# Two remainder tiles of 64 rows become one of 64 and one of 32, and the second one's weights are fetched at another point

## The chip, the cores and the metric

The kernel runs on one core of a Trainium2 chip. Its time is the device time of one execution in microseconds (us), and several executions are timed. The engines of the core work in parallel, each through its own queue in order: TensorE (PE; its weight loads are listed apart as PEld), VectorE (DVE), ScalarE (ACT), GpSimd (POOL) and SyncE (SP), which here issues most DMA transfers.

## The reference

A linear attention with decay feeds a mixture-of-experts layer in which every token goes to exactly one expert.

```
for b in range(nb):                                  # 12 blocks of 64 tokens, state carried along
    intra = (q @ k.T * Dmask) @ v ; inter = (q * lam_pow) @ kv_state
    kv_state = lam_block * kv_state + (k * rev_pow).T @ v
x = attention output as [3072 tokens, 512]
logits = x @ w_gate + modality_bias[modality_id]
e_idx = argmax(logits) ; gate_w = softmax(logits)[e_idx]
for e in range(8):                                   # w1[e]: 512x1024, w2[e]: 1024x512
    mask = e_idx == e
    out[mask] = gate_w[mask] * (relu(x[mask] @ w1[e]) @ w2[e])
```

With the seeded inputs, running the reference gives 1319, 253, 1494 and 6 tokens to experts 3, 5, 6 and 7, and none to the others. In tiles of 256 that is 5 full tiles and 39 left, 253 left, 5 full and 214 left, and 6 left.

## The kernel before

The first stage walks over 24 chunks of 128 tokens and computes attention, the logits and, for each token, a slot in a list sorted by expert (`inv` in DRAM). The tokens' rows go to `xs` in DRAM.

The second stage works on tiles of up to 256 rows of one expert. A **wide** tile (256 rows) gathers its rows with POOL's indirect DMA into `xg`, turns them on PE, splits rows and weights into a high and a low part (`split`: ACT casts, DVE subtracts; `xh`/`xl`, `w1h`/`w1l`, `w2h`/`w2l`) and takes three matmuls for each product (lines 554, 557, 558): `wide` is the first product, `second` the second. A **thin** tile takes a remainder of few rows. It multiplies in plain float32 and skips the splits. Its two halves of the hidden columns sit in the two 64-column halves of the PE array (`thin_first`, L584; `thin_turn`, L593; `thin_second`, L606).

Tiles 0 and 1 (`EARLY`) are wide and known after half of the tokens (`listA`). Tiles 2 and 3 are the thin ones, tiles 4 to 13 are wide and always run, and more follow under `tc.If`. All from tile 2 on come from `listB`, which `late_list` computes on DVE from the counts while tile 0 runs: a remainder of 1 to 64 rows counts as `few`, the first two such become thin, and every other remainder is rounded up to a wide tile.

Weights land in `raw1` (w1) and `raw2` (w2), 4 loads of 512 KB each; a load that would bring the expert already there is issued with a condition and moves nothing. The second thin tile cannot use them, since they hold the first one's weights: `fetch_both` (L643) loads its w1 into the buffers of `w1h` and its w2 into those of `w1l`, in `run_early`, once tile 1's first product no longer needs these. SP issues in program order. Ahead of those loads it stands at tile 2's w1 loads (L814, L531), which have an explicit wait for the last row gather that `run(0)` issued (`gathered`).

The order on PE around this: tile 1's first product, the transposes of thin tile 2's rows (`turn_few`, L640), tile 1's second product, those of thin tile 3's rows, `thin_first` of both, then `thin_turn`, half of `turn_rows` for tile 4 and `thin_second` for one thin tile after the other, then tile 4's first product. A scheduler orders what nothing in the code ties.

Of the kernel before, what the change touches and what calls it, by code (L numbers as in the profile page):

```python
# [15 lines left out]
P = 128  # L16
# [10 lines left out]
THIN = 2  # L27
# [5 lines left out]
LIST = THIN + MAX_WIDE + 2  # L33
# [5 lines left out]
def linear_attention_moe(tc, qkv, lam, modality, wg, mbias, w1, w2, out):  # L39
    nc = tc.nc  # L40
    with ExitStack() as ctx:
# [379 lines left out]
        def late_list(exA, nA):  # L421
# [10 lines left out]
            upto = const.tile([1, E, E], F32, name="upto")  # L432
            nc.vector.tensor_tensor(out=upto, in0=tri, in1=few.unsqueeze(1).to_broadcast([1, E, E]), op=ALU.mult)
            nth = per_expert("nth")
            nc.vector.tensor_reduce(out=nth, in_=upto, axis=AX, op=ALU.add)
            thins = per_expert("thins")
            nc.vector.scalar_tensor_tensor(out=thins, in0=nth, scalar=float(THIN), in1=few, op0=ALU.is_le, op1=ALU.mult)
# [3 lines left out]
            nc.vector.tensor_tensor(out=wides, in0=wides, in1=thins, op=ALU.subtract)  # L441
# [6 lines left out]
            for nm, num, skip, items in (("T", thins, n2, THIN), ("B", wides, nA, LIST - THIN)):  # L448
                base = const.tile([1, E + 1], F32, name="base" + nm)
                nc.vector.memset(base[:, E:], 0.0)  # L450
                nc.vector.tensor_tensor(out=base[:, :E], in0=ebase, in1=skip, op=ALU.add)
                delta = per_expert("delta" + nm)
                nc.vector.tensor_tensor(out=delta, in0=base[:, 1:], in1=base[:, :E], op=ALU.subtract)
                nc.vector.tensor_tensor(out=delta, in0=delta, in1=num, op=ALU.subtract)
                ends, ex, at = tile_list(num, delta, base[:, 0:1], items, nm)
                here = const.tile([1, items], F32, name="here" + nm)
                nc.vector.tensor_scalar(out=here, in0=sidx[:, :items], scalar1=ends[:, E - 1 :], scalar2=None, op0=ALU.is_lt)
# [3 lines left out]
                if nm == "T":  # L461
                    for i, o in enumerate((0, LIST - 1)):
                        prev, own = exs[:, 0:1], exs[:, o + 1 : o + 2]
                        nc.vector.tensor_tensor(out=own, in0=ex[:, i : i + 1], in1=prev, op=ALU.subtract)
                        nc.vector.scalar_tensor_tensor(out=own, in0=own, scalar=here[:, i : i + 1], in1=prev,
                                                       op0=ALU.mult, op1=ALU.add)
                        nc.vector.tensor_copy(out=ats[:, o : o + 1], in_=at[:, i : i + 1])
                        nc.vector.tensor_copy(out=others[:, o : o + 1], in_=here[:, i : i + 1])
                else:
                    nc.vector.tensor_scalar(out=exs[:, 2:LIST], in0=ex, scalar1=float(E - 1), scalar2=None, op0=ALU.min)  # L470
                    nc.vector.tensor_copy(out=ats[:, 1 : LIST - 1], in_=at)
                    nc.vector.tensor_copy(out=others[:, 1 : LIST - 1], in_=here)
# [56 lines left out]
        def fetch_w1(er, kw, after=None):  # L529
            for i in range(4):  # L530
                ld = nc.sync.dma_start(out=raw1[i], in_=w1[bass.ds(er, 1), :, i].rearrange("o p k f -> p (o k) f"), **kw)  # L531
                if after is not None:
                    behind(ld, after)

        def fetch_w2(er, kw, after=None):
            for i in range(4):
                ld = nc.sync.dma_start(out=raw2[i], in_=w2[bass.ds(er, 1), :, 2 * i : 2 * i + 2].rearrange("o p f n -> p (o f) n"), **kw)
                if after is not None:
                    behind(ld, after)
# [38 lines left out]
        def thin_first(x, w):  # L578

            hp = ps.tile([P, 2, TT], F32, name="s", bufs=3)  # L580
            for q in range(2):
                for kc in range(KC):
                    for fh in range(2):
                        mm = nc.tensor.matmul(hp[fh * XT : (fh + 1) * XT, q, :], x[:, kc, :], w[2 * fh + q][:, kc, :],  # L584
                                              start=(kc == 0), stop=(kc == KC - 1))
            hn = work.tile([P, 2 * TT], F32, name="hn", bufs=THIN)
            nc.scalar.activation(out=hn, in_=hp.rearrange("p q t -> p (q t)"), func=AF.Relu)
            return hn, mm

        def thin_turn(hn, mm):  # L590
            tp = ps.tile([P, 4, P], F32, name="x", bufs=2)
            for f in range(4):
                behind(nc.tensor.transpose(out=tp[:, f, :], in_=hn[:, f * P : (f + 1) * P], identity=ident), mm, wait=False)  # L593
            hnt = work.tile([P, 4, P], F32, name="hnt", bufs=THIN)
# [3 lines left out]
        def thin_second(idx, hnt, w2):  # L598

            w = DM // 2  # L600
            yp = ps.tile([P, w], F32, name="o", bufs=2)
            for f in range(FC):
                a, b = divmod(f, 2)
                fh, f4 = divmod(f, 4)
# [3 lines left out]
            y = work.tile([P, w], F32, name="yn", bufs=THIN)  # L608
            nc.scalar.activation(out=y, in_=yp, func=AF.Copy, scale=idx[:, 0, 1:2].bitcast(F32))
            to = work.tile([P, 1], I32, name="to", bufs=THIN)  # L610
            nc.vector.tensor_scalar(out=to, in0=idx[:, 0, 0:1], scalar1=2.0, scalar2=half, op0=ALU.mult, op1=ALU.add)
            sc = nc.gpsimd.indirect_dma_start(
                out=out.rearrange("t (n w) -> (t n) w", n=2),
                out_offset=bass.IndirectOffsetOnAxis(ap=to, axis=0),
                in_=y, in_offset=None, bounds_check=2 * N - 1, oob_is_err=False)
# [21 lines left out]
        def turn_few(x, rows):  # L637
            tp = ps.tile([P, KC, XT], F32, name="x", bufs=2)
            for kc in range(KC):
                nc.tensor.transpose(out=tp[:, kc, :], in_=rows[:, kc * P : (kc + 1) * P], identity=ident[:XT, :XT])  # L640
            return nc.vector.tensor_copy(out=x, in_=tp)

        def fetch_both(er, kw):  # L643

            first, second = parts(F32)
            for i in range(4):
                nc.sync.dma_start(out=first[i], in_=w1[bass.ds(er, 1), :, i].rearrange("o p k f -> p (o k) f"), **kw)
            second = [t.rearrange("p k f -> p (k f)").rearrange("p (f n) -> p f n", f=2) for t in second]
            for i in range(4):
                nc.sync.dma_start(out=second[i],  # L650
                                  in_=w2[bass.ds(er, 1), :, 2 * i : 2 * i + 2].rearrange("o p f n -> p (o f) n"), **kw)
            return first, second
# [4 lines left out]
        def parts(dt):  # L657

            return [[work.tile([P, KC, TT], dt, name=f"{nm}{i}", bufs=1) for i in range(4)] for nm in ("w1h", "w1l")]

        w1h, w1l = parts(F32R)
        xg = [const.tile([m, DM], F32, name=f"xg{t}") for t, m in groups(TT)]
        xq = [const.tile([XT, DM], F32, name=f"xq{i}") for i in range(THIN)]
# [4 lines left out]
        xf = [const.tile([P, KC, XT], F32, name=f"xf{i}") for i in range(THIN)]  # L668
        idxA = [const.tile([P, 2, 2], I32, name=f"idxA{i}") for i in range(EARLY)]
        half = const.tile([P, 1], F32, name="half")  # L670
        nc.vector.memset(half, 0.0)
        nc.vector.memset(half[XT:], 1.0)
# [29 lines left out]
        for g in range(0, ng + 2):  # L702
# [50 lines left out]
            elif g == ng + 1:  # L753
                for i in range(1, 4):
# [5 lines left out]
                    (work.tile([P, 4, 2, DM], F32R, name=nm, tag="load", bufs=LOADS) for nm in ("w2h", "w2l")))  # L760
        hh = [work.tile([P, 2, TT], F32R, name=f"hh{i}", tag="pt", bufs=4) for i in range(4)]
# [4 lines left out]
        tiles = [(TT, listA, i) for i in range(EARLY)] + [(XT, listB, 0), (XT, listB, LIST - 1)]  # L766
# [12 lines left out]
        fixed_ones = EARLY + THIN + MIN_WIDE  # L779
        wides = EARLY + THIN  # L780
# [3 lines left out]
        def rows_of(n):  # L784
# [5 lines left out]
            return fetch_rows(idxs[n], XT, to=[xq[n - EARLY]])  # L790

        def run(n):
# [5 lines left out]
            if n + 1 < fixed_ones:  # L798
# [5 lines left out]
                if n > 0:  # L804
                    fetch_w2(*regs(n + 1))
                turn_rows(TT, turned)
                for m in ahead:
                    gathered = rows_of(m)
                if ahead:
                    behind(nc.gpsimd.drain(), gathered, wait=False)  # L810
                for i in range(4):
                    split(raw1[i], w1h[i], w1l[i])
                if n + 2 < fixed_ones:
                    fetch_w1(*regs(n + 2), gathered)  # L814
            second(idx)

        def run_early(n):

            nonlocal w1h, w1l, before
# [12 lines left out]
            mm = thin_second(idxs[EARLY], hnt[0], raw2)  # L832
# [4 lines left out]
            before = thin_second(idxs[EARLY + 1], hnt[1], both[1])  # L837
            w1h, w1l = parts(F32R)
# [11 lines left out]
        with ExitStack() as nest:  # L850
            for n in range(fixed_ones, len(tiles)):
                nest.enter_context(tc.If(count > n - EARLY - THIN))
# [61 lines left out]
```

## Time and profile before

| | us |
|---|---|
| median of 3 timed runs | 424.17 |
| lowest and highest | 424.06, 426.81 |
| the profiled execution: its time | 426.98 |
| its span, first to last instruction | 425.2 |
| PE busy in it | 411.0 (97%) |
| DVE, ACT, POOL busy | 246.0, 187.5, 100.5 |
| mean granted TensorE clock | 0.996 of full |

The rows further below come from that execution. Times in them count from the start of its span. Its time is 1.78 us more than its span and 2.81 us more than the median.

### The profile page before, as it was taken

The page shows a single profiled execution, that of the slowest core. Times are in us where ns is not written, and L with a number is a line of the kernel's source. Part 1 is how long each engine was busy: PE and PEld are TensorE (multiplying, and loading weights), DVE is VectorE, ACT ScalarE, POOL GpSimd, SP SyncE. Part 2 cuts the span into 40 slices and gives each one's busy share as a digit, 9 for nine tenths or more (in the row PEclk, how much of TensorE's full clock was granted, in tenths as well). Part 3 has the DMA queues.
Part 4 walks back from the last instruction along what each step waited for, and adds up shares of the span by engine and source line. Part 5 has one row for each costly group of instructions (what it writes and reads, how often), then busy time and mean ns, then how long its engine had stood idle before and what let it go on. Part 6 is the DMA issues. An engine that isn't in the chain of part 4 may idle for free.

```text
span 425.2 us, 9463 instructions
## 1 busy us (share of the span) xinstructions
PE 411.0 (97%) x3636; PEld 360.5 (85%) x3636; DVE 246.0 (58%) x481; ACT 187.5 (44%) x298; POOL 100.5 (24%) x110
## 2 busy tenths in 40 slices
PE   8999999999989999799999999999999999999994
PEld 4787888888879897479898989999898989898983
DVE  4595968777379870157574563819092836547240
ACT  1222334233377151147473654637281827455330
POOL 3110143623430742022202031111112020200101
PEclk9999999999999999999999999999999999999998
DMA  5999989899930024901204577711102020100101
GB/s 161 399 333 377 344 306 308 253 340 313 376 103 3 27 52 111 368 11 50 77 25 145 186 213 251 226 71 37 65 4 72 26 74 28 66 26 2 51 1 47
DMA packets 35092, 63.00 MB, mean 148 GB/s; under 512 B 7381, under 2 KB 21213, under 8 KB 35040
## 3 DMA queue, kind: packets, MB, share of 16 engines
q1 hardware_dynamic: 17024, 43.08, 29.6%
q0 software_dynamic: 4800, 12.69, 9.0%
q10 hardware_dynamic: 13216, 6.56, 5.2%
q8 instruction: 30, 0.49, 0.5%
q14 instruction: 22, 0.18, 0.2%
HBM read 91.04 MB, written 13.75 MB: 246 GB/s over the span
## 4 chain that ended last, share of the span: by engine, by line
issue 43%; PE 30%; DMA 12%; POOL 7%; POOLq 2%; DVE 2%; SPq 2%; ACT 0%
PE s L224 6%; PE x L285 5%; DMA load<-in_qkv_dram 5%; PE o L273 5%; DMA idx<-inv 4%; POOL out_dram L628 4%; DMA xg<-xs,idx 3%; POOL xg L514 3%; PE o L262 2%; POOLq L810 2%; PE kv L239 2%; PE o L554 2%; PE o L557 2%; PE o L558 2%; PE s L558 2%
## 5 line engine op out<-in xcount | busy, mean ns | idle before, releaser
L554 PE MATMUL s<-xh,w1h 128*128 128x256 f32 x384 | 108.2, 282 | 0.8 <-issue 0.8
L558 PE MATMUL s<-xh,w1l 128*128 128x256 f32 x384 | 108.0, 281 | 0.3 <-DVE w1l L487 0.3
L557 PE MATMUL s<-xl,w1h 128*128 128x256 f32 x384 | 107.9, 281 | 0.0
L487 DVE TENSOR_TENSOR w1l<-raw,w1h 128x1024 fp32r<-128x1024 f32 x48 | 58.1, 1219 | 82.2 <-ACT w1h L486 81.4
L554 PE MATMUL o<-w2h,hh 128*128 128x512 f32 x192 | 75.9, 395 | 0.0
L558 PE MATMUL o<-w2h,hl 128*128 128x512 f32 x192 | 74.9, 390 | 0.0
L557 PE MATMUL o<-w2l,hh 128*128 128x512 f32 x192 | 74.7, 389 | 0.0
L554 PEld LDWEIGHTS s<-xh,w1h 128*128 128x128 f32 x384 | 72.3, 188 | 1.8 <-issue 1.4
L558 PEld LDWEIGHTS s<-xh,w1l 128*128 128x128 f32 x384 | 72.3, 188 | 0.5 <-DVE w1l L487 0.5
L557 PEld LDWEIGHTS s<-xl,w1h 128*128 128x128 f32 x384 | 72.4, 188 | 0.4
L486 ACT CAST w1h<-raw 128x1024 fp32r<-128x1024 f32 x48 | 49.9, 1052 | 24.7 <-PE s L557 24.7
L487 DVE TENSOR_TENSOR w2l<-raw,w2h 128x1024 fp32r<-128x1024 f32 x48 | 58.4, 1217 | 2.1 <-ACT w2h L486 2.0
L486 ACT CAST w2h<-raw 128x1024 fp32r<-128x1024 f32 x48 | 49.9, 1041 | 0.0
L627 ACT ACTIVATE y<-o,idx 128x512 f32<-128x512 f32 x20 | 13.8, 690 | 77.4 <-PE o L558 44.2
L628 POOL DMA_INDIRECT out_dram<-y,idx x20 | 20.3, 1013 | 106.9 <-ACT y L627 95.6
L514 POOL DMA_INDIRECT xg<-xs,idx x20 | 24.1, 1203 | 83.7 <-PE x L547 80.0
L573 DVE SCALAR_TENSOR_TENSOR hl<-s,hh 128x512 fp32r<-128x512 f32 x48 | 32.8, 684 | 17.0 <-ACT hh L572 17.0
L558 PEld LDWEIGHTS o<-w2h,hl 128*128 128x128 f32 x192 | 36.0, 188 | 7.7
L554 PEld LDWEIGHTS o<-w2h,hh 128*128 128x128 f32 x192 | 36.1, 188 | 7.1
L557 PEld LDWEIGHTS o<-w2l,hh 128*128 128x128 f32 x192 | 36.1, 188 | 7.0
L275 ACT COPY xt<-o 128x256 f32<-128x256 f32 x48 | 17.5, 373 | 51.8 <-PE o L273 47.1
L572 ACT ACTIVATE hh<-s 128x512 fp32r<-128x512 f32 x48 | 28.5, 594 | 16.9 <-PE s L558 16.9
(192 smaller groups left out, 495.5 us busy)
## 6 DMA issues: line engine op xcount, KB each, us to landing
raw<-in_w_dram SPq DMA_DIRECT2D x104, 512.0 KB
load<-in_qkv_dram SPq DMA_DIRECT2D x11, 2048.0 KB
xs<-xn ACTq DMA_DIRECT2D x24, 256.0 KB
load<-in_qkv_dram SPq DMA_DIRECT2D x4, 512.0 KB
w1h<-in_w_dram SPq DMA_DIRECT2D x4, 512.0 KB
w1l<-in_w_dram SPq DMA_DIRECT2D x4, 512.0 KB
inv<-pad SPq DMA_DIRECT2D x2, 196.0 KB
inv<-pad SPq DMA_DIRECT2D x2, 192.0 KB
```

Of the source, the lines that this page charges most:

```text
L224: nc.tensor.matmul(sps[hl][:, p, :], kt[r, p, :], qt[r, p, :], start=True, stop=True)
L273: mm = nc.tensor.matmul(op[half][place(p, hl), i, :], vt[:, (2 * p + hl) * D : (2 * p + hl + 1) * D], pts[hl][:, p, :], start=(c == 0 and ...
L285: nc.tensor.matmul(xp[:, j, : P + E], xt[:, p, :], iw[:, p, :], start=True, stop=True)
L486: cp = nc.scalar.copy(out=hi, in_=src)
L487: df = nc.vector.tensor_tensor(out=lo, in0=src, in1=hi.bitcast(F32), op=ALU.subtract)
L514: last = nc.gpsimd.indirect_dma_start(out=(to or xg)[t][:m], out_offset=None, in_=xs[:rows, :], in_offset=bass.IndirectOffsetOnAxis(ap=idx ...
L554: mm = nc.tensor.matmul(out, ah, bh, start=first, stop=False)
L557: nc.tensor.matmul(out, ah, bl, start=False, stop=False)
L558: return nc.tensor.matmul(out, al, bh, start=False, stop=last)
L572: act = nc.scalar.activation(out=hh[i], in_=hp, func=AF.Relu)
L573: nc.vector.scalar_tensor_tensor(out=hl[i], in0=hp, scalar=0.0, in1=hh[i].bitcast(F32), op0=ALU.max, op1=ALU.subtract)
L628: sc = nc.gpsimd.indirect_dma_start(out=out, out_offset=bass.IndirectOffsetOnAxis(ap=idx[:, t, 0:1], axis=0), in_=y, in_offset=None, bound ...
```

## The change

`THIN` becomes `(64, 32)`: thin tile 2 holds up to 64 rows and thin tile 3 up to 32. `late_list` sorts the remainders by size; a 32-row remainder may also take the first place if no larger one wants it. A remainder for which no place is left becomes a wide tile, as before. A 32-row tile uses four column groups of 32 of the PE array. Its first product is 16 matmuls of 256 columns (16 before), its second is 32 of 128 columns (16 of 256 before), and two transposes stand between them (four before).

The second thin tile's w2 goes to `spare`, a third buffer of the attention stage's load pool, and is fetched in `run(0)`. Its w1 still goes to the `w1h` buffers, and is fetched first in `run_early`. `w1l` is no longer used for it. Tile 2's w1 loads lose the wait for the gather.

```diff
-THIN = 2
+THIN = (P // 2, P // 4)
...
             few = per_expert("few")
             nc.vector.tensor_scalar(out=few, in0=rem, scalar1=0.0, scalar2=None, op0=ALU.is_gt)
-            upto = const.tile([1, E, E], F32, name="upto")
...
-            nc.vector.scalar_tensor_tensor(out=thins, in0=nth, scalar=float(THIN), in1=few, op0=ALU.is_le, op1=ALU.mult)
+            nc.vector.scalar_tensor_tensor(out=size[:, 1], in0=rem, scalar=float(THIN[1]), in1=few, op0=ALU.is_le,
+                                           op1=ALU.mult)
+            nc.vector.tensor_tensor(out=size[:, 0], in0=few, in1=size[:, 1], op=ALU.subtract)
...
-        def fetch_w1(er, kw, after=None):
+        def fetch_w1(er, kw, after=None, to=None):
...
         def thin_first(x, w):
-            hp = ps.tile([P, 2, TT], F32, name="s", bufs=3)
-            for q in range(2):
+            m = x.shape[-1]
+            n = P // m
+            hp = ps.tile([P, 4 // n, TT], F32, name="s", bufs=3)
+            for q in range(4 // n):
                 for kc in range(KC):
-                    for fh in range(2):
-                        mm = nc.tensor.matmul(hp[fh * XT : (fh + 1) * XT, q, :], x[:, kc, :], w[2 * fh + q][:, kc, :],
+                    for fh in range(n):
+                        mm = nc.tensor.matmul(hp[fh * m : (fh + 1) * m, q, :], x[:, kc, :], w[4 // n * fh + q][:, kc, :],
...
-        def thin_second(idx, hnt, w2):
-            w = DM // 2
+        def thin_second(m, idx, hnt, w2):
+            n = P // m
+            w = DM // n
...
-                for j in range(2):
-                    mm = nc.tensor.matmul(yp[j * XT : (j + 1) * XT], hnt[:, f4, fh * XT : (fh + 1) * XT],
+                for j in range(n):
+                    mm = nc.tensor.matmul(yp[j * m : (j + 1) * m], hnt[:, f4, fh * m : (fh + 1) * m],
                                      w2[a][:, b, j * w : (j + 1) * w], start=(f == 0), stop=(f == FC - 1))
...
+        spare = work.tile([P, 4, 2, DM], F32, name="spare", tag="load", bufs=LOADS)
...
         def run(n):
...
                     idxs[m] = get_idx(m)
                 if n > 0:
                     fetch_w2(*regs(n + 1))
+                else:
+                    fetch_w2(*fetch_regs(*tiles[EARLY + 1][1:], True), to=spare)
...
-                    fetch_w1(*regs(n + 2), gathered)
+                    fetch_w1(*regs(n + 2), gathered if n > 0 else None)
...
         def run_early(n):
...
             wide(tail)
+            few1 = parts("w1h", F32)
+            fetch_w1(*fetch_regs(*tiles[EARLY + 1][1:], True), to=few1)
             fetch_w2(*regs(EARLY))
-            both = fetch_both(*fetch_regs(*tiles[EARLY + 1][1:], True))
             turn_few(xf[0], xq[0])
             second(idx)
             turn_few(xf[1], xq[1])
             hn, _ = thin_first(xf[0], raw1)
             fetch_w1(*regs(wides))
-            other, mm = thin_first(xf[1], both[0])
+            other, mm = thin_first(xf[1], few1)
...
-            before = thin_second(idxs[EARLY + 1], hnt[1], both[1])
-            w1h, w1l = parts(F32R)
+            before = thin_second(THIN[1], idxs[EARLY + 1], hnt[1], spare)
+            w1h = parts("w1h", F32R)
```

On SP, from the index loads of the thin tiles on. Before (`raw` is w1 in `raw_121` to `124` and w2 in `raw_125` to `128`; `w1h` and `w1l` are tile 3's weights):

```order
L502 DMA idx_2156<-inv 64x2 [waits DMAHW4_49,DMASW3_49]
...
L502 DMA idx_2168<-inv 64x2 [waits DMAHW6_49]
...
L504 DMA idx_2180<-inv 128x2x2 [waits DMAHW0_49]
...
L531 DMA raw_121<-in_w_dram 128x1024 [waits DMAHW1_49,DMASW1_49]
...
L537 DMA raw_125<-in_w_dram 128x1024 [waits DMAHW5_49,DVE_49]
...
L647 DMA w1h_2455<-in_w_dram 128x1024 [waits DMAHW1_49,PE_49]
...
L650 DMA w1l_2459<-in_w_dram 128x1024 [waits DMAHW5_49]
```

After, the same stretch on SP:

```order
L536 DMA idx_2166<-inv 64x2 [waits DMAHW4_49,DMASW3_49]
...
L536 DMA idx_2178<-inv 32x2 [waits DMAHW6_49]
...
L536 DMA idx_2178<-inv 32x2 [waits DMAHW1_49]
...
L538 DMA idx_2192<-inv 128x2x2 [waits DMAHW2_49]
...
L571 DMA spare<-in_w_dram 128x1024 [waits DMAHW3_49,PE_49]
...
L565 DMA raw_121<-in_w_dram 128x1024 [waits DMAHW7_49]
...
L565 DMA w1h_2449<-in_w_dram 128x1024 [waits DMAHW3_49,PE_49]
...
L571 DMA raw_125<-in_w_dram 128x1024 [waits DMAHW7_49,DVE_49]
```

Tile 3's index list takes four loads for two, its w2 (`spare`) moves ahead of tile 2's w1, which no longer waits for a gather (DMASW), and its w1 moves ahead of tile 2's w2. The first `w1h` load shares a semaphore (DMAHW3) with the first `spare` load.

On PE, thin tile 3 and what stands round it. Before (`xf_150` are its rows, `hnt` its turned hidden values, `w1h` and `w1l` its weights):

```order
L640 MATMUL x<-ident,xq_140 128x64 x4
...
L584 MATMUL s<-w1h_2455,xf_150 64x256
...
L606 MATMUL o<-raw_128,hnt 64x256 x4
L593 MATMUL x<-ident,hn 128x128 x4
...
L606 MATMUL o<-w1l_2459,hnt 64x256 x4
```

After, at the same places on PE:

```order
L679 MATMUL x<-ident,xq_140 128x32 x4
...
L620 MATMUL s<-w1h_2449,xf_150 32x256
...
L644 MATMUL o<-raw_128,hnt_2625 64x256 x4
L630 MATMUL x<-ident,hn_2618 128x128 x2
...
L644 MATMUL o<-spare,hnt_2661 32x128 x32
```

The places are the same; what changes is the width of the column group, the number of transposes and the count and length of the second product's matmuls.

## Rows read from the trace of the kernel before

**Rows 1.** Stretches: their bounds, length, busy us (instructions) of each engine, clock, DMA share, GB/s.
```profile
168.29:178.41 10.12, 7.91 (x66) 4.59 (x64) 0.42 (x1) 1.05 (x2) 1.01 (x1) 1.00 0.98 367
...
188.50:211.60 23.10, 23.10 (x154) 21.22 (x153) 15.63 (x17) 12.90 (x17) 6.61 (x6) 1.00 0.21 59
```

**Rows 2.** Timeline of PE, thin tiles: start, us, instruction, [idle before, releaser].
```profile
168.29 3.67 PE L584 MATMUL s<-raw,xf 128*64 128x256 f32 x32
171.79 0.59 PE L584 MATMUL s<-w1h,xf 128*64 128x256 f32 x2
173.80 1.95 PE L584 MATMUL s<-w1h,xf 128*64 128x256 f32 x16 [1.41 <-DMA w1h<-in_w_dram]
176.54 1.94 PE L584 MATMUL s<-w1h,xf 128*64 128x256 f32 x14 [0.80 <-DMA w1h<-in_w_dram]
178.41 0.66 PE L593 MATMUL x<-ident,hn 128*128 128x128 f32 x4
...
179.86 3.67 PE L606 MATMUL o<-raw,hnt 128*64 128x256 f32 x32 [0.35 <-DVE hnt L595]
183.46 0.65 PE L593 MATMUL x<-ident,hn 128*128 128x128 f32 x4
183.95 0.60 PE L547 MATMUL x<-ident,xg 128*128 128x128 f32 x4
184.90 3.67 PE L606 MATMUL o<-w1l,hnt 128*64 128x256 f32 x32 [0.35 <-DVE hnt L595]
...
188.84 0.28 PE L558 MATMUL s<-xh,w1l 128*128 128x256 f32 x1
```

**Rows 3.** Timeline of SP's DMA issues (a group's time includes its waits).
```profile
149.39 3.14 SPq L502 DMA_DIRECT2D idx<-inv  x4
...
162.60 1.69 SPq L531 DMA_DIRECT2D raw<-in_w_dram  x4
...
166.21 2.10 SPq L647 DMA_DIRECT2D w1h<-in_w_dram  x4
```

**Rows 4.** Timeline of PE in the attention stage: matmuls on 64 by 64 cells.
```profile
97.23 0.67 PE L262 MATMUL o<-qd,state 64*64 64x128 f32 x16
97.83 1.09 PE L273 MATMUL o<-pt,load 128*64 128x128 f32 x16
```

**Rows 5.** Timeline of DVE: row copy, turned copy, low part of the next weights.
```profile
168.40 0.42 DVE L641 COPY xf<-x 128x256 f32<-128x256 f32 x1 [9.09 <-PE x L640]
...
184.15 0.69 DVE L595 COPY hnt<-x 128x512 f32<-128x512 f32 x1 [3.30 <-PE x L593]
...
186.15 3.50 DVE L487 TENSOR_TENSOR w1l<-raw,w1h 128x1024 fp32r<-128x1024 f32 x3 [0.26 <-ACT w1h L486]
```

**Rows 6.** Timeline of ACT: high part of the next weights.
```profile
185.07 2.94 ACT L486 CAST w1h<-raw 128x1024 fp32r<-128x1024 f32 x3
```

**Rows 7.** Timeline of DVE: start, the end of the list, tile 1's first low part.
```profile
11.17 1.29 DVE L227 TENSOR_TENSOR pt<-s,dk 128x512 f32<-128x512 f32 x2 [4.86 <-DMA dk<-tab_d]
...
147.25 0.17 DVE L474 TENSOR_SCALAR listB<-ats 1x21 int32<-1x21 f32 x1
150.04 0.69 DVE L573 SCALAR_TENSOR_TENSOR hl<-s,hh 128x512 fp32r<-128x512 f32 x1 [2.63 <-ACT hh L572]
```

**Rows 8.** Timeline of POOL: the first thin gather, tile 4's first scatter.
```profile
153.34 0.99 POOL L514 DMA_INDIRECT xq<-xs,idx  x1 [5.02 <-DMA idx<-inv]
...
207.49 1.04 POOL L628 DMA_INDIRECT out_dram<-y,idx  x1 [4.01 <-ACT y L627]
```

**Rows 9.** Timeline of PE where thin tile 2's rows are turned.
```profile
156.20 0.28 PE L558 MATMUL s<-xh,w1l 128*128 128x256 f32 x1
156.41 0.46 PE L640 MATMUL x<-ident,xq 64*128 64x64 f32 x4
```

**Rows 10.** DMA, 154.5 to 156.4 us: all that moved.
```profile
DMA packets 160, 0.08 MB, mean 43 GB/s; under 512 B 140, under 2 KB 140, under 8 KB 160
```

**Rows 11.** DMA, 156.4 to 158.2 us: all that moved.
```profile
DMA packets 48, 0.01 MB, mean 7 GB/s; under 512 B 45, under 2 KB 45, under 8 KB 48
```

More of the change, by code (lines that the diff above doesn't have):

```diff
@@ L440, in late_list @@
             nc.vector.tensor_tensor(out=wides, in0=wides, in1=few, op=ALU.add)
-            nc.vector.tensor_tensor(out=wides, in0=wides, in1=thins, op=ALU.subtract)
+            for i in range(2):
+                nc.vector.tensor_tensor(out=wides, in0=wides, in1=thins[:, i], op=ALU.subtract)
             exs = const.tile([1, LIST + 1], F32, name="exs")
@@ L447, in late_list, with only @@
             others = const.tile([1, LIST], F32, name="others")
[L448 to L457, printed above, removed]
+            def only(here, at):
@@ L459, in late_list @@
                 nc.vector.scalar_tensor_tensor(out=at, in0=at, scalar=float(EMPTY), in1=here, op0=ALU.subtract, op1=ALU.mult)
                 nc.vector.tensor_scalar(out=at, in0=at, scalar1=float(EMPTY), scalar2=None, op0=ALU.add)
[L461 to L472, printed above, removed]
+            base = const.tile([1, E + 1], F32, name="baseB")
@@ new lines, in late_list @@
+            nc.vector.memset(base[:, E:], 0.0)
+            nc.vector.tensor_tensor(out=base[:, :E], in0=ebase, in1=nA, op=ALU.add)
+            delta = per_expert("deltaB")
+            nc.vector.tensor_tensor(out=delta, in0=base[:, 1:], in1=base[:, :E], op=ALU.subtract)
+            nc.vector.tensor_tensor(out=delta, in0=delta, in1=wides, op=ALU.subtract)
+            items = LIST - len(THIN)
+            ends, ex, at = tile_list(wides, delta, base[:, 0:1], items, "B")
+            here = const.tile([1, items], F32, name="hereB")
@@ new lines, in late_list @@
+            nc.vector.tensor_scalar(out=here, in0=sidx[:, :items], scalar1=ends[:, E - 1 :], scalar2=None, op0=ALU.is_lt)
+            only(here, at)
+            nc.vector.tensor_scalar(out=exs[:, 2:LIST], in0=ex, scalar1=float(E - 1), scalar2=None, op0=ALU.min)
+            nc.vector.tensor_copy(out=ats[:, 1 : LIST - 1], in_=at)
+            nc.vector.tensor_copy(out=others[:, 1 : LIST - 1], in_=here)
+            tail_at = per_expert("tail_at")
+            nc.vector.tensor_tensor(out=tail_at, in0=ebase, in1=n2, op=ALU.add)
@@ new lines, in late_list @@
+            sh = [1, 2, E]
+            found = []
+            for nm, what in (("is", None), ("ex", sidx[:, :E]), ("at", tail_at)):
+                v = thins
+                if what is not None:
+                    v = const.tile(sh, F32, name="pick" + nm)
+                    nc.vector.tensor_tensor(out=v, in0=thins, in1=what.unsqueeze(1).to_broadcast(sh), op=ALU.mult)
+                got = const.tile([1, 2], F32, name="got" + nm)
+                nc.vector.tensor_reduce(out=got, in_=v, axis=AX, op=ALU.add)
+                found.append(got)
@@ new lines, in late_list @@
+            here, ex, at = found
+            only(here, at)
+            for i, o in enumerate((0, LIST - 1)):
+                prev, own = exs[:, 0:1], exs[:, o + 1 : o + 2]
+                nc.vector.tensor_tensor(out=own, in0=ex[:, i : i + 1], in1=prev, op=ALU.subtract)
+                nc.vector.scalar_tensor_tensor(out=own, in0=own, scalar=here[:, i : i + 1], in1=prev,
+                                               op0=ALU.mult, op1=ALU.add)
+                nc.vector.tensor_copy(out=ats[:, o : o + 1], in_=at[:, i : i + 1])
+                nc.vector.tensor_copy(out=others[:, o : o + 1], in_=here[:, i : i + 1])
@@ L637, in turn_few, with parts @@
         def turn_few(x, rows):
-            tp = ps.tile([P, KC, XT], F32, name="x", bufs=2)
+            m = x.shape[-1]
+            tp = ps.tile([P, KC, m], F32, name="x", bufs=2)
             for kc in range(KC):
-                nc.tensor.transpose(out=tp[:, kc, :], in_=rows[:, kc * P : (kc + 1) * P], identity=ident[:XT, :XT])
+                nc.tensor.transpose(out=tp[:, kc, :], in_=rows[:, kc * P : (kc + 1) * P], identity=ident[:m, :m])
             return nc.vector.tensor_copy(out=x, in_=tp)
[L643 to L652, printed above, removed]
         raw1 = [const.tile([P, KC, TT], F32, name=f"raw1{i}") for i in range(4)]
         raw2 = [const.tile([P, 2, DM], F32, name=f"raw2{i}") for i in range(4)]
-        def parts(dt):
-            return [[work.tile([P, KC, TT], dt, name=f"{nm}{i}", bufs=1) for i in range(4)] for nm in ("w1h", "w1l")]
-        w1h, w1l = parts(F32R)
+        def parts(nm, dt):
+            return [work.tile([P, KC, TT], dt, name=f"{nm}{i}", bufs=1) for i in range(4)]
+        w1h, w1l = parts("w1h", F32R), parts("w1l", F32R)
         xg = [const.tile([m, DM], F32, name=f"xg{t}") for t, m in groups(TT)]
-        xq = [const.tile([XT, DM], F32, name=f"xq{i}") for i in range(THIN)]
+        xq = [const.tile([m, DM], F32, name=f"xq{i}") for i, m in enumerate(THIN)]
         for x in xg + xq:
```

80 lines of the change are left out of this document (48 added, 32 removed).

## The prediction

> **What bounds the kernel now.** I read the busy shares first: PE works 411.0 of 425.2 us, so the kernel is a chain of matmuls, and only what PE does or waits for counts. The table of stretches then says where the chain has slack. A wide tile such as the one from 188.50 to 211.60 keeps PE busy for all of its 23.10 us, while the 10.12 us from 168.29 on have PE busy for 7.91 and the DMA engines for 98% [rows 1]. The reader should see there a stage of its own, in which transfers, not matmuls, end last. The granted clock is 1.00 in both stretches [rows 1], so it is no term of the sum.
>
> PE's timeline opens that stage. The first thin tile's first product runs from 168.29 to 171.79: 32 matmul instructions in 3.50 us, 109 ns apart. The second thin tile's same product begins at 171.79 and gives way to the transposes only at 178.41, after 6.62 us [rows 2]. The rows name the weights in `w1h` as what it waited for, 1.41 and 0.80 us; the other 0.91 of the 3.12 us of excess is restarting behind each stop. SP's timeline says why they are late: SP reaches these loads at 166.21, because at 162.60 it was still held in tile 2's w1 loads, by the row gather [rows 3]. From there both matrices of the second thin tile, 4.2 MB, share the DMA engines at 367 GB/s [rows 1].
>
> **First product of the second thin tile.** The change keeps 32 instructions of 256 columns, but on 32 of the 128 columns of the array. In the 64-column form two run side by side, 109 ns apart [rows 2]. If four run side by side, they are 55 ns apart and the product takes 1.75 us; if still only two, 3.50 us. No row shows four column groups that read the same 128 partitions. I take 1.75, because the form nearest to it, two groups, shows no loss, and keep 3.50 as the other end. With weights in time: 6.62 - 1.75 = 4.87 us saved.
>
> Three column groups of 32 gained a factor of 2.38 rather than 3 in a measurement that the Trainium skill gives ("TensorE: Matmul & The Clock Gate", part 3 on packing small matmuls). No run here shows it; four groups at that efficiency would gain 3.17, an estimate by which this product takes 2.2 us and the whole change gives 418.1.
>
> **Are the weights in time?** Four index loads take 3.14 us of SP [rows 3], 0.78 each. Now there are six, and one for tile 4: from 149.39 until about 154.9. The four loads of `spare`, at 0.53 each (2.10 us for four [rows 3]), go out by 157.0, tile 2's conditional ones (1.69 us [rows 3], less the wait) by 158.7, and the w1 loads after that. Each matrix is 2.1 MB, 5.7 us at 367 GB/s [rows 1]. `spare` lands by about 162, and as each w1 load shares a semaphore with a `spare` load and waits for it, w1 lands by about 168. PE needs it at 171.79 [rows 2]: some 4 us in hand, so the stall goes whole.
>
> **Turning between the products.** From 183.46 to 184.90 there are 1.44 us: four transposes (0.49 until 183.95), the transposes of tile 4's rows, and the rest of a wait for the 0.69 us copy of `hnt` [rows 2, 5]. Two transposes fewer save 0.25, and the copy of half the size should cost the 0.42 of the 128x256 copy [rows 5], 0.27 less. That makes 0.92, 0.52 saved.
>
> **Second product.** It takes 3.60 us now (179.86 to 183.46, the first thin tile's [rows 2]). It becomes 64 instructions of 128 columns. Four side by side without loss would be 27 ns apart, 1.75 us in all. Two side by side, as in the attention stage's 128*64 matmuls, are 55 to 68 ns apart (1.09 us for 16 with the last one's tail [rows 4]), 3.5 to 4.4 us. The nearest row is that stage's 64*64 form, which fills four groups of cells: 16 in 0.60 us (97.23 to 97.83 [rows 4]), 37.5 ns apart. At that, 2.40 us, 1.20 saved.
>
> **What is late next.** Tile 4's first product needs `w1l`. ACT's first cast for it starts at 185.07 [rows 6], DVE's subtraction at 186.15, and one takes 1.17 us (3.50 for three [rows 5]), so it stands at 187.32, 3.86 us after the transposes began at 183.46. These casts wait for tile 4's turned rows, which come 0.25 us sooner: 3.61. PE would want it 0.92 + 2.40 + 0.34 = 3.66 us after the same point (the 0.34 from 188.50, where the second product's 3.60 us end, to 188.84 [rows 2]). So ACT and DVE just keep up: a second product quicker than 2.40 us would gain nothing more.
>
> **At nothing.** The list on DVE grows by four instructions of some 0.17 us [rows 7]. DVE is idle for 2.63 us behind it [rows 7]. The sharper edge is SP, which reads the list, loads the indices at 149.39, so that POOL can gather at 153.34 [rows 3, 8]; that gather moves in the stretch up to 156.4 [rows 10], and PE turns the rows at 156.41, 0.21 us behind the matmul before [rows 9]. There are a few tenths in hand at most: price between 0 and 0.7 us, taken as 0, since SP reads one list entry less ahead of the load. DVE's output address for tile 3 waits for two index loads more, about 1.6 us; behind it stand tile 1's last low parts, which PE reads only in the second half of the product it starts at 156.41 plus the transposes. On POOL, tile 6's gather now stands behind tile 4's first scatter (207.49 [rows 8]), but its rows are turned only behind tile 5's first product, which starts at 211.60 [rows 1]. Four memsets more at the start lie between the steps of a chain of dependent multiplications whose result DVE awaits at 11.17 [rows 7]; 0.2 us at most. All later tiles are bound by PE and only move forward.
>
> **The sum.** 4.87 + 0.52 + 1.20 = 6.59 us. The profiled execution would go from 426.98 to 420.4, its span to 418.6. That execution lies 2.81 us over the median, so from the median: 424.17 - 6.6 = **417.6**, 1.6% faster. Differences under about 1%, 4.2 us, can't be told from no change here.
>
> **Rivals.**
> *Only two column groups at a time* (chance 0.21). The array may be unable to stream four float32 operands out of the same partitions; the 64*64 form, with two groups per row half, already falls from 27 to 37.5 ns [rows 4]. Against it speaks the loss-free pairing in the thin tiles [rows 2]. Then the first product stays at 3.50, the second at 3.60 or so, and what remains is 3.12 + 0.52 = 3.6 us: 420.5, within 1%.
> *The weights don't come earlier* (0.03): the chain from `spare` to `w1h` on SP and the semaphores, with gathers in between, eats the 4 us, and the 3.12 us stall stays. Then 3.5 us are gained: 420.7, within 1%.
> *The list delays the first thin gather* (0.05): PE waits ahead of tile 1's second product, up to 0.7 us and as much again by the gather sharing the DMA engines with `spare`; 419.0, still faster.
> *Slower: an eleventh wide tile* (0.03). With places of 64 and 32, two remainders of 33 to 64 rows no longer both fit, and the second becomes a wide tile, 23.10 us [rows 1], while the stall still goes: 424.17 + 23.1 - 6.6 = 440.7. It decides once the smaller remainder exceeds 32 rows. The reference's counts leave 39 and 6, and the gathers agree: 0.08 MB is 39 rows of 2 KB, 0.01 MB is 6 [rows 10, 11].
>
> **Numbers.** The forecast holds 0.68. The two cases near 420.6 hold 0.24, so the range runs from 416.9 (a few tenths below the forecast for the spread of runs, since ACT and DVE cap the gain) to 420.8. Faster by over 1%: 0.68 + 0.05 = 0.73; within 1%: 0.24; slower: 0.03.
>
> **What would show it.** In the changed profile the second thin tile's first product should take about 1.75 us with no wait for DMA on `w1h`; 3.5 us without a wait means that groups of 32 pair only by two. Its second product should take 2.4 us and the 128x256 copy of `hnt` 0.42. The third matmul of tile 4 should start near 182.2; a wait for `w1l` there means ACT and DVE cap the gain. The first `w1h` load on SP should stand near 159 to 162. A gap ahead of the thin rows' transposes near 156.4 means the list or the gather is late, and four `w1h` casts more would mean another wide tile. The forecast is wrong if PE gains idle time behind 182 us.

## The result, and the profile after

In the first measurement the changed kernel takes 419.59 us (median of four runs, 418.97 to 420.36) against 424.56 us before, 5.0 us less between the medians; the ratio is 0.987 [0.983, 0.991], that is 5.3 us (3.6 to 7.1). Two later measurements, beside more runs of the kernel before, gave 0.983 [0.979, 0.986] and 0.985 [0.981, 0.990]. The time lies in the predicted range, 2.0 us above the forecast of 417.6, but two terms of the sum were wrong and cancel in part, as the experiments show.

The profiled execution after takes 419.86 us, its span 418.1, where those of before were 426.98 and 425.2. PE's timeline in the thin stage, beside [rows 2] and [rows 9] (start, us, instruction, count, idle time before and what ended it):

```profile
156.65 0.46 PE L679 MATMUL x<-ident,xq 64*128 64x64 f32 x4 [0.85 <-DMA xq<-xs,idx]
168.16 0.43 PE L679 MATMUL x<-ident,xq 32*128 32x32 f32 x4
168.52 3.67 PE L620 MATMUL s<-raw,xf 128*64 128x256 f32 x32
172.12 1.93 PE L620 MATMUL s<-w1h,xf 128*32 128x256 f32 x32
173.99 0.66 PE L630 MATMUL x<-ident,hn 128*128 128x128 f32 x4
...
175.42 3.67 PE L644 MATMUL o<-raw,hnt 128*64 128x256 f32 x32 [0.34 <-DVE hnt L632]
179.03 0.44 PE L630 MATMUL x<-ident,hn 128*128 128x128 f32 x2
179.30 0.60 PE L581 MATMUL x<-ident,xg 128*128 128x128 f32 x4
179.98 1.95 PE L644 MATMUL o<-spare,hnt 128*32 128x128 f32 x64
181.87 0.38 PE L588 MATMUL s<-xh,w1h 128*128 128x256 f32 x1
...
182.79 0.38 PE L592 MATMUL s<-xh,w1l 128*128 128x256 f32 x1 [0.43 <-DVE w1l L521]
...
205.66 0.28 PE L588 MATMUL s<-xh,w1h 128*128 128x256 f32 x1
```

The second thin tile's first product runs from 172.12 to 173.99 without a stop: 1.87 us, not 6.62. Its second product ends where tile 4 begins, at 181.87: 1.89 us, not 3.60. The third matmul of tile 4 stands at 182.79, not 188.84, behind a new wait of 0.43 us for `w1l`. A second new wait, 0.85 us for the rows `xq`, stands ahead of the first thin transposes.

SP's DMA issues, beside [rows 3] (a group's time includes its waits):

```profile
148.00 3.88 SPq L536 DMA_DIRECT2D idx<-inv  x6
...
153.31 1.94 SPq L571 DMA_DIRECT2D spare<-in_w_dram  x4
156.15 1.32 SPq L565 DMA_DIRECT2D raw<-in_w_dram  x4
158.32 5.09 SPq L565 DMA_DIRECT2D w1h<-in_w_dram  x4
```

The first load of `w1h` is reached at 158.32 instead of 166.21.

To see where the whole 7.1 us between these two spans came from, I cut them at the first thin transposes and at tile 5's first matmul. Up to the transposes: 156.41 before, 156.65 after. From there to tile 5: 55.36 before (to 211.77), 49.01 after (to 205.66), so 6.35 saved. From tile 5 to the end: 213.43 before, 212.44 after, so 1.0 saved where I had expected nothing. 6.35 + 0.99 - 0.24 = 7.1. Two questions were left: why the medians differ by only 5.0, and why tiles that the diff does not touch became quicker.

### The profile page after: what moved, and what is told of

It is laid out like the page before. It is cut to its first block, busy times and chain, and to the rows that moved or that the text cites. A ratio compares the mean times of both kernels' runs of the same rounds, so it can differ in the third digit from the quotient of the medians.

```text
span 418.1 us, 9536 instructions
## 1 busy us (share of the span) xinstructions
PE 404.6 (97%) x3665; PEld 356.4 (85%) x3666; DVE 245.9 (59%) x487; ACT 188.4 (45%) x298; POOL 100.0 (24%) x110
## 4 chain that ended last, share of the span: by engine, by line
issue 44%; PE 22%; DMA 13%; POOL 8%; DVE 6%; POOLq 3%; SPq 3%; ACT 1%; DVEq 0%; ACTq 0%
PE s L224 6%; PE x L285 5%; DMA load<-in_qkv_dram 5%; PE o L273 5%; DMA idx<-inv 4%; POOL out_dram L666 4%; POOL xg L548 3%; DMA xg<-xs,idx 3%; POOLq L844 2%; PE o L262 2%; PE kv L239 2%; DVE w1l L521 1%; SPq L565 1%; DVE w2l L521 1%; PE s L592 1%
```

## The experiments

Each measurement set its kernels beside runs of the kernel before on the same chip. That kernel's median was 426.98 us beside the first four, 424.44 beside the next four and 427.24 beside the last four, so ratios are compared, not times. The first and the last four ran on one chip, the next four on another; the change as it stands was not timed on that other one.

**The change again, and `spare` fetched later.** The first is the changed kernel itself. The second moves one fetch behind the small tile's w1:

```diff
-                else:
-                    fetch_w2(*fetch_regs(*tiles[EARLY + 1][1:], True), to=spare)
...
+            few_er, few_kw = fetch_regs(*tiles[EARLY + 1][1:], True)
+            fetch_w1(few_er, few_kw, to=few1)
+            fetch_w2(few_er, few_kw, to=spare)
```

> The changed kernel once more, beside the experiments on the same chip. By the steps of its trace it should be 5 to 6 us faster than the kernel before: 6.3 us less between the transposes of the second thin tile's rows and the third matmul of tile 4, less the 0.85 us that PE waited for the first thin gather. If instead the 7.1 us by which the two spans differ are the change's, 7 us.

> spare is fetched in run_early, behind the second thin tile's w1, and no longer in run(0). Theory: spare's 2.1 MB and the first thin gather shared the DMA engines, and that is why PE waited 0.85 us for the rows of the first thin tile; the wait falls to 0.1 us or less, spare still lands some 10 us before it is read, and the kernel is 0.8 us faster than the changed one. Rival: the longer list and the two more index loads made the gather late; the wait stays at 0.6 to 0.9 us and the time is the changed kernel's.

Measured: 420.4 us, ratio 0.983 [0.979, 0.986], and 420.22 us, 0.982 [0.980, 0.985]. Neither profile has a wait for `xq`, so the 0.85 us belongs to single executions, and moving the fetch is worth nothing that can be told: the 0.8 us foreseen for it did not come.

**The order alone.** Two 64-row tiles, with the change's list, its `spare` and its order of fetches:

```diff
-THIN = (P // 2, P // 4)
+THIN = (P // 2, P // 2)
...
-            hn = work.tile([P, F // n], F32, name=f"hn{m}", bufs=1)
+            hn = work.tile([P, F // n], F32, name=f"hn{m}", bufs=2)
...
```

> Both thin tiles are of 64 rows, as before the change; list code, spare and the order of the fetches are the change's. Theory, that the transfers and the column groups each pay their own part: the second thin tile's first product runs without a DMA wait in 3.5 us (6.6 before), its second product stays at 3.6, the wait of 0.85 us for the first gather is there; 3.1 - 0.85 = 2.3 us faster than before. Rival, that the earlier weights are the whole gain: 5 us faster.

Measured: 427.91 us, ratio 1.000 [0.998, 1.003], so neither the 2.3 nor the 5 us came. Its profiled execution is the longest of its runs, so only what happens there is read from it, not how large it is on average. PE's timeline, and a table of stretches (bounds, length, busy us and instructions of PE, PEld, DVE, ACT and POOL, granted clock, DMA share, GB/s):

```profile
162.34 0.68 PE L679 MATMUL x<-ident,xq 64*128 64x64 f32 x4 [3.51 <-DMA xq<-xs,idx]
176.73 0.46 PE L679 MATMUL x<-ident,xq 64*128 64x64 f32 x4
```

```profile
158.00:161.00 3.00, 0.84 (x8) 0.63 (x6) 1.38 (x2) 1.14 (x2) 2.39 (x3) 1.00 0.94 325
161.00:164.00 3.00, 1.66 (x7) 1.35 (x8) 0.93 (x2) 0.39 (x1) 0.60 (x1) 0.65 1.00 376
164.00:167.00 3.00, 3.00 (x9) 2.32 (x8) 1.22 (x2) 0.00 (x0) 0.00 (x0) 0.50 1.03 407
167.00:170.00 3.00, 3.00 (x11) 2.40 (x10) 0.00 (x0) 0.00 (x0) 0.00 (x0) 0.71 0.95 373
```

The gather on POOL, and the loads of `spare` on SP:

```profile
156.26 0.98 POOL L548 DMA_INDIRECT xq<-xs,idx  x1 [5.50 <-DMA idx<-inv]
```

```profile
156.29 2.02 SPq L571 DMA_DIRECT2D spare<-in_w_dram  x4
```

Here the rival on the gather came true, at 2.5 times its price (0.7 and as much again): PE waits 3.51 us for `xq` while the DMA engines are 94 to 100% busy, mostly with weights. The gather was issued together with the loads of `spare`, and PE had its rows 6.1 us later (162.34); in three profiles of the change it was issued 0.7 to 1.3 us ahead of them, and PE had them within 4.1 us. With one such profile this order is a likely cause, not a shown one. Behind the idle time the granted clock falls to 0.50, the 1.2 GHz level, and tile 1's second product takes 14.39 us between the two groups of transposes, where it took 11.49 before (156.41 to 167.90).

**The size alone.** Tiles of 64 and 32 rows, their weights fetched as before, into `w1h` and `w1l` and behind the row gather:

```diff
-                    fetch_w1(*regs(n + 2), gathered if n > 0 else None)
+                    fetch_w1(*regs(n + 2), gathered)
...
-            few1 = parts("w1h", F32)
+            few1, few2 = parts("w1h", F32), parts("w1l", F32)
...
+            fetch_w2(few_er, few_kw, to=few2)
```

> The tiles are of 64 and 32 rows, but the second one's weights are fetched as before the change: w1 into w1h and w2 into w1l, behind tile 2's loads, which wait for the row gather. Theory: in the 32-column form each step of the first product reads all four quarters of w1, so it can't start before the last one lands (176.5 in the trace of before) and ends at 178.4, as before: no gain there. The turn gains 0.5 and the second product 1.7, of which tile 4's w1l lets through 1.7 in all; 1.7 us faster than before, no wait for the first gather. Rival, that the two parts simply add: 1.7 more from the first product, 3.5 us faster.

Measured: 424.35 us, ratio 0.992 [0.990, 0.995]. PE's timeline:

```profile
173.89 0.62 PE L620 MATMUL s<-w1h,xf 128*32 128x256 f32 x4
174.81 0.62 PE L620 MATMUL s<-w1h,xf 128*32 128x256 f32 x2 [0.29 <-DMA w1h<-in_w_dram]
176.99 1.91 PE L620 MATMUL s<-w1h,xf 128*32 128x256 f32 x26 [1.56 <-DMA w1h<-in_w_dram]
178.83 0.66 PE L630 MATMUL x<-ident,hn 128*128 128x128 f32 x4
```

The product takes 4.94 us, with the wait for weights in it. The size alone gains 0.8%, the changed kernel beside it 1.7%: with the small tile, early weights do pay. The 0.8%, 2.6 us between the medians, lies between the two expectations (1.7 and 3.5 us), and some 1.3 us of it are not the size's: the later tiles of this kernel run at the change's pace, and its `w1h` lies at the change's place (last group below).

**The order without the collision, and the row gather's wait alone.** The first is the order alone with `spare` late, as above. The second is the kernel before with one condition more:

```diff
-                    fetch_w1(*regs(n + 2), gathered)
+                    fetch_w1(*regs(n + 2), gathered if n > 0 else None)
```

> Two 64-row tiles with the change's list and order of fetches, but the spare weights fetched behind the ones for the first product, not ahead of the first thin gather. Theory (the order has a worth of its own, and the run with the order alone lost it to the 2 MB of spare that shared the DMA engines with the first thin gather): the wait for xq (3.51 us there) is below 0.3 us, the granted clock does not fall behind it, the second thin tile's first product takes 3.5 to 3.6 us without a wait for weights (6.62 us before), and the kernel is 2.6 to 3.6 us faster than before, ratio 0.992 to 0.994. Rival (the order has no worth without the small second tile, since what the earlier weights give is lost at the next wait): ratio 0.998 to 1.002, and a wait of 2 us or more turns up at tile 4's products.

> The kernel before, in which only the loads of weights behind tile 0 no longer wait for the gather of rows. Theory (this wait is one part of what held up the second thin tile's weights): the loads of w1h start near 164.5 us instead of 166.2, the second thin tile's first product shrinks from 6.62 to about 4.9 us, the kernel is 1.4 to 1.9 us faster, ratio 0.9955 to 0.9968. Rival A (the queue is held by the next buffer to come free and not by the gather): the loads of w1h start where they did within 0.3 us, ratio 0.999 to 1.001. Rival B (the wait kept the gather free of the loads): PE waits over 0.8 us for xq, and the kernel is no faster.

Measured: 423.24 us, ratio 0.997 [0.995, 0.999], and 423.97 us, 0.999 [0.997, 1.001]. PE's timeline of the first:

```profile
170.25 3.62 PE L620 MATMUL s<-w1h,xf 128*64 128x256 f32 x32
173.81 0.66 PE L630 MATMUL x<-ident,hn 128*128 128x128 f32 x4
```

SP's DMA issues of the second:

```profile
153.39 1.30 SPq L531 DMA_DIRECT2D raw<-in_w_dram  x4
...
160.37 2.52 SPq L647 DMA_DIRECT2D w1h<-in_w_dram  x4
```

In the two profiles the product takes 3.56 and 3.55 us without a wait, the full 3.1 us less than in [rows 2], and SP reaches `w1h` at 154.45 and 160.37 instead of 166.21. In the second, tile 2's loads stand at 153.39 instead of 162.60, so the row gather was what held SP there, as the prediction read it, and rival A is out. Yet the runs gain 1.2 and 0.5 us. Both expectations fail on the time, and my reading of that wait with them: on this chip the kernel before does not lose 3 us there on average.

**The kernel before, once more.**

> The kernel before, unchanged, profiled in another execution. Theory (the 3.0 us for which the second thin tile's first product waited for w1h belong to single executions: with the addresses shifted, and without the gather wait, that wait was not there, and neither edit made the kernel faster by that much): this product takes 3.5 to 4.5 us here, and from the first thin transposes to the first matmul of tile 4 it is 29.0 to 30.0 us instead of 32.09. Rival (the wait is part of every execution of this kernel, and the shift took it away): 6 us or more, and 31.5 to 32.5 us from the transposes to tile 4.

PE's timeline:

```profile
156.21 0.46 PE L640 MATMUL x<-ident,xq 64*128 64x64 f32 x4 [0.16 <-issue]
...
168.77 3.67 PE L584 MATMUL s<-raw,xf 128*64 128x256 f32 x32
172.27 3.94 PE L584 MATMUL s<-w1h,xf 128*64 128x256 f32 x32
176.15 0.66 PE L593 MATMUL x<-ident,hn 128*128 128x128 f32 x4
...
209.49 0.28 PE L554 MATMUL s<-xh,w1h 128*128 128x256 f32 x1
```

Where SP reaches the loads of `w1h` in this execution, then in the kernel before with an unused tile of 192 bytes (the last group below):

```profile
165.32 2.02 SPq L647 DMA_DIRECT2D w1h<-in_w_dram  x4
```

```profile
164.94 2.10 SPq L647 DMA_DIRECT2D w1h<-in_w_dram  x4
```

The same program has the product done in 3.88 us here, 0.33 more than without a wait, so the 3 us of waiting in [rows 2] are not in every execution. From the transposes to tile 4's first matmul (186.24) it is 30.03 us, not 32.09; the gain is smaller than that of the product because a wait of 0.39 us for `w2l` in tile 1's second product takes some back. What differs is how far SP is ahead: it reaches `w1h` 5.58 us before PE begins the product in [rows 2] (166.21 and 171.79), 6.95 us here, and 7.02 us with the 192 bytes, where PE begins at 171.96 and nothing waits. This execution took 424.93 us, its span 423.2, and the 2.0 us between the two spans are all in the stretch from the transposes to tile 5 (55.36 and 53.28 us). It was also the shortest of its eight, whose median is 426.76 us; no profile shows how many of the others wait.

**The change, and both small waits taken out.** In the second kernel `spare` is late, and the first two quarters of tile 4's weights are split earlier:

```diff
+            w1h = parts("w1h", F32R)
+            for i in range(2):
+                cast, low = split(raw1[i], w1h[i], w1l[i])
+            mm = thin_second(THIN[0], idxs[EARLY], hnt[0], raw2, cast)
...
-            for i in range(4):
+            for i in range(2, 4):
```

> The changed kernel, unchanged, beside the next kernel and the kernel before. Theory (3.84 us from the small tile, 1.35 us from the pace of the later tiles, 0.3 to 0.9 us given back at the waits for xq and w1l, and up to 3 us more where the kernel before had to wait for w1h): 4.2 to 7.2 us faster than before, ratio 0.983 to 0.990. Rival (the wait for w1h is the larger part of the gain in each execution): 6.5 us or more in each batch, ratio below 0.985.

> The changed kernel with two edits: spare is fetched behind the small tile's first weights and no longer ahead of the first thin gather, and the first two quarters of tile 4's weights are split ahead of the second thin tile's last product. Theory: no wait for xq, no wait for w1l at tile 4 (0.31 to 0.43 us before), so 0.3 to 0.4 us faster than the changed kernel, up to 1.2 us where that one waits for xq; against before a ratio lower by 0.001 to 0.003. Rival (ACT and DVE have no room for the early splits, so that the hnt copies and the splits of xg come later): the waits move to the second product of the thin tiles or to x, and the time is the changed kernel's or up to 0.5 us more.

Measured: 420.16 us, ratio 0.985 [0.981, 0.990], and 421.8 us, 0.989 [0.986, 0.992]. The change is within its expectation; the other kernel is not. The change's span here is 156.84 up to the transposes (0.55 of it a wait for `xq`), 49.04 to tile 5, 212.42 behind. Against the kernel before just shown (156.21, 53.28, 213.71) that is 4.9 us in all: 4.24 in the stage, 1.29 behind it, 0.63 given back ahead.

The other kernel's PE timeline:

```profile
179.57 1.69 PE L647 MATMUL o<-spare,hnt 128*32 128x128 f32 x48
181.57 0.42 PE L647 MATMUL o<-spare,hnt 128*32 128x128 f32 x5 [0.32 <-issue]
182.33 0.43 PE L647 MATMUL o<-spare,hnt 128*32 128x128 f32 x5 [0.33 <-issue]
183.08 0.42 PE L647 MATMUL o<-spare,hnt 128*32 128x128 f32 x5 [0.32 <-issue]
183.82 0.27 PE L647 MATMUL o<-spare,hnt 128*32 128x128 f32 x1 [0.32 <-issue]
```

Both waits are gone (no idle time ahead of `xq` at 156.20 nor at tile 4's third matmul), but the second product now takes 4.45 us, because PE stands four times for 0.32 or 0.33 us, and the profile shows nothing that it waits for. What holds it there is open. It was not better than the change, so the change stays the fastest version tried, with `spare` late level with it.

**Where the buffers of weights lie.** In each profile the first product of a later wide tile, 96 matmuls, takes either 11.36, 11.31 or 11.21 us, at a granted clock of 1.00. With the 32-row tile and the new list, the work buffers, `w1h` and `w1l` among them, lie 320 bytes lower in each partition: `w1h` at 143392, not 143712. Three kernels do nothing but add an unused tile ahead of them, of 320, 192 and 64 bytes:

```diff
         nums = const.tile([1, 1], I32, name="nums")
+        const.tile([P, 80], F32, name="shift")   # changed kernel; 16 for 64 bytes
+        const.tile([P, 48], F32, name="shift")   # kernel before
```

> The changed kernel with one unused tile of 320 bytes per partition ahead of the buffers of weights, so that w1h, w1l, the second weights, hh and hl lie at the addresses that they have in the kernel before (w1h at 143712 instead of 143392). Theory (where these buffers lie sets the pace of the wide tiles' first product): that product takes 11.36 us in each later wide tile instead of 11.21, the period is 23.14 instead of 22.99, and over nine periods the kernel is 1.2 to 1.5 us slower than the changed kernel, so only 5.0 to 6.5 us faster than before where the changed kernel was 6.5 to 7.5. Rival (something else of the small tile, the code's place or its list, sets the pace): 11.21 and 22.99 stay, and the time is that of the changed kernel within 0.5 us.

> The kernel before with one unused tile of 192 bytes per partition ahead of the buffers of weights: w1h at 143904 instead of 143712, 32 bytes past a multiple of 512 as in the changed kernel, where it was 352 past. Nothing else is changed. Theory (addresses set the pace, by their place in a line of 512 bytes or a divisor of it): the wide tiles' first product takes 11.21 us instead of 11.36, and the kernel is 1.2 to 1.5 us faster, ratio 0.9965 to 0.9972. Rival (pace set by something else): 11.36 stays, ratio 0.999 to 1.001. A pace between (11.31, as with the order alone, where w1h lay at a multiple of 512) would say that addresses matter but not by this remainder.

> The changed kernel with an unused tile of 64 bytes per partition ahead of the buffers of weights: w1h at 143456, which is 96 past a multiple of 128, as in the kernel before (143712), and 96 past a multiple of 512, where that one is 352 past. If the place within 128 bytes sets the pace, the wide tiles' first product takes 11.36 us; if the place within 512 bytes or more does, it takes something else than 11.36, 11.21 if only some places cost anything.

The product's length is the distance between these two rows of PE's timeline, for one later tile: before, then after, then the changed kernel shifted by 320 bytes, the kernel before shifted by 192, and the changed kernel shifted by 64.

```profile
281.19 0.28 PE L554 MATMUL s<-xh,w1h 128*128 128x256 f32 x1
292.55 0.71 PE L547 MATMUL x<-ident,xg 128*128 128x128 f32 x5
```

```profile
297.63 0.28 PE L588 MATMUL s<-xh,w1h 128*128 128x256 f32 x1
308.84 0.38 PE L581 MATMUL x<-ident,xg 128*128 128x128 f32 x2
```

```profile
298.76 0.28 PE L588 MATMUL s<-xh,w1h 128*128 128x256 f32 x1
310.12 1.04 PE L581 MATMUL x<-ident,xg 128*128 128x128 f32 x8
```

```profile
300.69 0.28 PE L554 MATMUL s<-xh,w1h 128*128 128x256 f32 x1
311.89 1.04 PE L547 MATMUL x<-ident,xg 128*128 128x128 f32 x8
```

```profile
301.97 0.28 PE L588 MATMUL s<-xh,w1h 128*128 128x256 f32 x1
313.33 0.93 PE L581 MATMUL x<-ident,xg 128*128 128x128 f32 x7
```

11.36, 11.21, 11.36, 11.20 and 11.36 us. An unused tile makes the changed kernel's wide tiles as slow as before, and another makes the old ones as quick as after. By place of `w1h`: 96 bytes past a multiple of 128 in each slow case, 32 past in each quick one, and 11.31 us with the order alone (143872, a multiple of 128). In time: the shifted kernel before took 423.03 us, ratio 0.996 [0.995, 0.998], 1.4 us faster without any change to its work; the shifted changed kernel 421.75, 0.993 [0.990, 0.995]; the third had one run, 424.9. That second ratio is 3.1 us (2.0 to 4.1), less than the 5.0 to 6.5 expected, which were reckoned from the other chip. Of the first product's operands only the stationary `w1h` and `w1l` move with the unused tile; `xh` and `xl` keep their addresses in all of these kernels, and the second product keeps its 10.99 us. So `w1h` and `w1l` are the likely ones, but other work buffers move with them, and no run moved them alone.

## Why the prediction was right, and where not

**What bounds the kernel: right.** PE's chain sets the time, and the saving came from its thin stage.

**First product, 4.87 us: right for the profiled execution, too much for the median.** 6.62 became 1.87, so 4.75 us. Four column groups of 32 do run side by side: 58 ns apart, where 55 was taken. The rival of two groups (3.50) is out. The Trainium skill's 2.38 for three groups ("TensorE: Matmul & The Clock Gate", part 3), carried over as an estimate, gave 2.2; the trace's four groups are quicker, at 3.50 / 1.87 = 1.87 times the rate of two.

The step that failed is the one behind the sum: "That execution lies 2.81 us over the median, so from the median". The wait for `w1h` was itself a large part of what lay over the median, so it could not be subtracted once more from the median. It is 3.1 us in one profile of the same program and 0.33 in the other, and taking away a cause of it gained 0.5 us (0.999 [0.997, 1.001], on the other chip). What the small tile surely saves in that product is 3.55 - 1.87 = 1.68.

**Weights in time: right.** SP reached `w1h` at 158.32 (predicted 158.7), and PE did not wait. Its worth depends on the execution: it removes a wait that the kernel before has in some, and that was still there with the size alone (1.85 us of idle time).

**Turn and second product: 1.72 us foreseen, 2.20 came.** The turn went from 1.44 to 0.95 (179.03 to 179.98), where 0.92 was worked out; the copy of `hnt` took the 0.42. The second product took 1.89 instead of 2.40: the 64*64 form of [rows 4] was the wrong neighbour, and the lossless end, 1.75, the better one.

**"ACT and DVE just keep up": the mechanism right.** What the second product gained more, they took back. DVE's timeline after, beside [rows 5]:

```profile
179.50 0.42 DVE L632 COPY hnt<-x 128x256 f32<-128x256 f32 x1 [3.08 <-PE x L630]
181.51 4.63 DVE L521 TENSOR_TENSOR w1l<-raw,w1h 128x1024 fp32r<-128x1024 f32 x4 [0.26 <-ACT w1h L520]
```

The first `w1l` ends 1.16 us (a fourth of 4.63) behind 181.51, at 182.67, 3.64 us after the transposes of 179.03; I had 3.61. PE was there 0.48 us earlier than assumed (0.95 + 1.89 + 0.34 = 3.18 us behind the same point, not 3.66) and waited 0.43. That is idle time behind 182 us, which the prediction had named as a sign that the forecast is wrong; it is small, and of the kind that the prediction described.

**The list and the gather, taken as 0: mostly right.** The wait for `xq` was 0.85, 0 and 0.55 us in three profiles of the change, and 0 with `spare` late. The first lies above the 0.7 us that was its highest price. Its larger form showed with the order alone, 3.51 us and a fallen clock.

**"All later tiles ... only move forward": wrong.** Each became 0.15 us shorter by the place of its weights, 1.0 to 1.3 us in all behind tile 5's start. This made up for less than half of what the wait was overrated by, so that the forecast came as near as it did is in part luck.

Put right: about 3.2 us of the size, some 1.3 of the place, 0 to 3.1 of the wait that the kernel before has or has not, less 0 to 0.85 for `xq`: 3.7 to 7.6 us. By their ratios the three measurements gave 5.3, 7.4 and 6.3.

The size's part is read from the first thin transposes to tile 5. The kernel before with the 192 bytes takes 52.20 us there without a wait for `w1h`, the change 49.01, its 0.43 for `w1l` included:

```profile
156.52 0.46 PE L640 MATMUL x<-ident,xq 64*128 64x64 f32 x4
...
171.96 3.62 PE L584 MATMUL s<-w1h,xf 128*64 128x256 f32 x32
...
208.72 0.28 PE L554 MATMUL s<-xh,w1h 128*128 128x256 f32 x1
```

In six profiles, of the change, of its two shifted forms and of the one with `spare` late, this stretch is 49.0 to 49.2 us. In time, the change at the old pace was 3.1 us faster than the kernel before on the other chip. How often the kernel before waits for `w1h`, and so how much of the 6.3 and 7.4 us is that wait, stays open.

## What to carry to other kernels

A wait in one profiled execution that lies well over the median is not to be subtracted from the median: profile the kernel a second time, or take the cause of the wait away and time it. When a change resizes any buffer, compare the pace of a product that the diff does not touch, since an unused tile of some dozen bytes can give or cost what looks like a gain of the change. Weights fetched early can compete with the small gathers that the same stage waits for; before moving a load forward, look in the trace whether the gather is issued ahead of it.

## What was not expected of the hardware

96 matmuls of the same form, at a granted clock of 1.00, took 11.36 or 11.21 us by where their buffers lay, 1.6 ns a matmul, with 96 and 32 bytes past a multiple of 128. After 3.51 us in which PE waited, the granted clock was at 0.50 in the next full stretch of 3 us. Float32 matmuls on 32 columns of the array ran four side by side at 1.87 times the rate of two groups of 64: 32 of 256 columns in 1.87 us instead of 3.50, and 64 of 128 columns in 1.89.
